# Q and K in seven output tiles, K's last four heads through the padding rows

## The chip, the core and the metric

The kernel runs on one NeuronCore of a Trainium2 chip. The metric is the device time of one execution in microseconds. The engines are TensorE (PE in the profile, with its weight loads as PEld), VectorE (DVE), ScalarE (ACT), GpSimd (POOL) and SyncE (SP), which issues most of the DMAs. Each engine works through its own queue in order and waits on semaphores of the others.

## The reference

A transformer block with conditioning, on 2048 tokens of width 448, in bf16:

```python
mod = (silu(c) @ w_mod)                 # six vectors: sa, ca, ga, sb, cb, gb
h = layernorm(x) * (1 + ca) + sa
# attention: 16 heads of 28; each token looks at 8 keys, itself and every second one before it
q, k, v = split(h @ wqkv)
o = softmax(q . k[pos - 2*w], w = 0..7) . v
x = x + ga * (o @ wo)
h = layernorm(x) * (1 + cb) + sb
x = x + gb * (silu(h @ w1) @ w2)        # 448 -> 1792 -> 448
```

## The kernel before

The 2048 tokens are cut into four chunks of 512 (256 positions of each parity, since attention looks only at keys of a token's own parity). Each chunk goes through layer norm, a transpose, Q, K and V projections, attention in blocks of 112 queries per parity (0 to 8, with 128 in block 0), the output projection, a second layer norm, and the two matrix products of the feed-forward part.

The code first records operations, each with a name, its engine, its dependencies and the buffers it takes, in a `Plan`; then it emits them in an order written out by hand, the string `ORDER`, in which a number is the operation's place of recording and a letter chooses ACT (`a`) or DVE (`v`) where either will do. Each engine's queue is the subsequence of `ORDER` that runs on it, so the order decides who stands behind whom. Names used here: `n1.2 T` is the transpose of chunk 2's first norm, `QK2.0.1` group 1 of chunk 2's Q and K, `V5` the values of block 5, `L3.0` the logits of block 3, parity 0, `exp` and `mask` what follows them, `AV3` attention times values, `onorm3` its division by the sums, `oT3` the transpose of the result, `WO1.0` the output projection, `x1` the residual add, `F1.0.2` tile pair 2 of chunk 0's first feed-forward product, `F2.0` a pair of rows of the second.

PSUM is used as four pairs of banks (`ps`). A projection takes one pair; a logits block takes two, and each is given back by its exp.

The contraction is over 448 = 3.5 x 128 rows. The helper `duo` fills two output tiles at once, with seven steps of two matmuls of 64 rows each that run side by side in the two halves of the array: three steps, then, after a `turn` (a wait on POOL's queue so that the halves may swap banks), four more, as two operations on PE. An eviction on ACT or DVE follows.

For Q and K a head's 28 columns are padded to 32, so that four heads fill the 128 rows of an output tile: rows 28 to 31 of every 32 are zero weights. Group g of 4 has a tile of Q and one of K (line 627), both evicted by one copy (line 630) into `qk`, whose dimensions are rows, Q or K, group, parity and position:

```python
w = wp[rows, kk, H * j + 4 * g:H * j + 4 * g + 4, :] if kk < 3 else wp3[rows, 4 * g:4 * g + 4, :]
return T.matmul(ps[:, j, 0:2 * n], lhsT=w.rearrange("p h d -> p (h d)"), rhs=h[rows, :, t, c0:c0 + n], start=start, stop=stop)
```

Chunk 0 comes in two parts of 256 columns, so that it can start early; the others have 512 columns. The padded weights `wp`, `wp3` are made by four `pad` copies from the loaded `wqk`, `wqk3` (lines 564 and 566). The space of `wqk` becomes later the normalised input of chunk 2, and `wqk3` and a part of `both` are scratch for sums of squares.

x of chunk 0 is loaded in two halves, `x0a` on SP's queue and `x0b` on ACT's; `c` follows on ACT's queue (line 368 issues all loads).

Of the kernel before, what the change touches and what calls it, by code (L numbers as in the profile page):

```python
# [15 lines left out]
D = 448  # L16
# [60 lines left out]
def half(j):  # L77
    return slice(K3 * j, K3 * j + K3)
# [33 lines left out]
def dram(ap, row, col, dims):  # L112

    w = ap.ap[0][0]
    return bass.AP(ap.tensor, ap.offset + row * w + col, [[r * w + c, n] for r, c, n in dims])

# [125 lines left out]
def layer(ctx, tc, io, safe):  # L242
# [13 lines left out]
    def ct(shape, name, dt=BF16):  # L256
        return const.tile(shape, dt, name=name)
# [15 lines left out]
    wp3 = ct([128, H, 32], "wp3")  # L273
    wo = ct([128, 2, KT, D], "wo")
# [16 lines left out]
    screp = ct([128, KT, 128], "screp")  # L291
# [78 lines left out]
    def first_x(i):  # L370
        return dict(out=x_all[:, 2 * i:2 * i + 2, :].rearrange("p t d -> p (t d)"), in_=x_view[0, :, i, :])
# [6 lines left out]
    ld_x = [[load(224, **first_x(0), run=1792, name="x0a"), load(224, **first_x(1), run=1792, q=nc.scalar, name="x0b")]]  # L378
    first = ld_x[0][0]["deps"][0]
    ld_c = [load(1, c4[0:3, :], c[:, 0:384].rearrange("o (k p) -> (o k) p", p=128), [ld_x[0][1]["deps"][0]], run=256, q=nc.scalar, name="c")]  # L380
# [11 lines left out]
    ld_qk = [[a], [b], [a], [load(56, wqk3[half(a), 0:D], A_wqkv[128 * (a + 1):128 * (a + 1) + K3, D * (1 - a):D * (2 - a)], late, name="wqk") for a in range(2)]]  # L392
# [6 lines left out]
    ld_1 += [load(112, w13[half(a), :], B_w1[128 * (a + 1):128 * (a + 1) + K3, F // 2 * (1 - a):F // 2 * (2 - a)], late, run=1792, name="w1") for a in range(2)]  # L399
# [161 lines left out]

    def pad(o, kk):
        if kk < 3:
            copy_on(o)(out=wp[:, kk, :, 0:DH], in_=wqk[:, kk, :].rearrange("p (h d) -> p h d", d=DH))
        else:
            copy_on(o)(out=wp3[:, :, 0:DH], in_=wqk3[:].rearrange("p (h d) -> p h d", d=DH))
# [28 lines left out]
    def norm1(k):  # L595
        h = h1[k % NH]
        after = [x for kk in (k - NH,) if kk >= 0 for x in qk_mm[kk] + v_mm[kk] + [halo[kk + 1]]] + (pads if k == 2 else [])
        if k == 0:
            parts = []
            for i in range(2):  # L600
                n = Norm([2 * i, 2 * i + 1], {2 * i + j: [ld_x[0][i]] for j in range(2)}, how=HOW1[0], tag=f"n1.0{i}")
                n.on_pe(lambda kk, i=i: h[:, :, kk, 128 + 128 * i:256 + 128 * i], [mod1])
                h1_norms.extend(n.done)
                parts.append(list(n.done))
            h1_done[0] = parts
            return
        n = Norm([4 * k + j for j in range(4)], {4 * k + j: [ld_x[k][j // 2]] + h1_norms[:1] for j in range(4)}, after=after, how=HOW1[k], tag=f"n1.{k}")
        n.on_dma(lambda j: h[:, :, :, 128 + 64 * j:256 + 64 * j].rearrange("p t k s -> p (t k) s"), lambda kk: h[:, :, kk, 128:128 + CP], 0, [mod1])
        h1_done[k] = [list(n.done)]
        w = 32 * k  # L610
        halo[k] = P.op(either(60.0 + 0.83 * 8 * w, 60.0 + 0.26 * 8 * w), lambda o: copy_on(o)(out=h[:, :, :, 128 - w:128].rearrange("p t k s -> p (t k) s"),
                                                                                           in_=h1[(k - 1) % NH][:, :, :, 128 + CP - w:128 + CP].rearrange("p t k s -> p (t k) s")),
                       h1_done[k - 1][-1] + after, name=f"halo{k}")

    def project(k):
# [3 lines left out]
        n = CP // len(parts)  # L619
        for i, ready in enumerate(parts):  # L620
            c0 = 128 + n * i
            s0 = CP * k + n * i
            done = []
            for g in range(4):
                def make(ps, j, kk, rows, t, start, stop, g=g, c0=c0):
                    w = wp[rows, kk, H * j + 4 * g:H * j + 4 * g + 4, :] if kk < 3 else wp3[rows, 4 * g:4 * g + 4, :]
                    return T.matmul(ps[:, j, 0:2 * n], lhsT=w.rearrange("p h d -> p (h d)"), rhs=h[rows, :, t, c0:c0 + n], start=start, stop=stop)  # L627

                def ev(o, ps, g=g, s0=s0):
                    copy_on(o)(out=qk[:, :, g, :, s0:s0 + n], in_=ps[:, :, 0:2 * n].rearrange("p j (t s) -> p j t s", t=2))  # L630
                m, e = duo(make, 2 * n, ready + pads, (either(act_ns(4 * n), dve_ns(4 * n)), ev, [], None), f"QK{k}.{i}.{g}")
                qk_mm[k] += m
                done.append(e)
            qk_done[k].append(done)
# [111 lines left out]
    def out_proj(k, i):  # L746
# [26 lines left out]
        for par in range(2):  # L773
            x1_done[u + par] = P.op(("dve", 545.0), lambda o, par=par: add(o, par), [m], name=f"x1.{u + par}")
# [224 lines left out]
```

## Time and profile before

| what | before |
|---|---|
| median of 3 runs (lowest to highest) | 171.43 us (171.3 to 171.44) |
| profiled execution | 171.64 us, span 169.9 us |
| PE busy | 162.0 us, 2015 matmuls |
| ACT busy | 114.5 us, 163 instructions |
| DVE busy | 96.1 us, 189 instructions |
| POOL busy | 33.2 us, 88 instructions |
| mean granted TensorE clock | 0.989 |

The span runs from the first instruction to the last. Busy time is the time in which an engine has an instruction in work; a matmul waiting inside its pipeline counts as busy, so a busy PE need not be at its full rate. A row of the timeline gives the start in the span, the length from the first start to the last end, the engine, the line, the operation, the tile written and the tiles read, the count, and in brackets the idle time before it with what ended it. Two rows of pipelined instructions can overlap at their ends, so the cost of a group is read from its start to the start of the next group.

### The profile page before, as it was taken

To read this page: it belongs to the slowest core of one execution; us is meant where nothing else is said; L and a number is where in the kernel's file an instruction comes from. 1 tells how busy PE (TensorE), PEld (TensorE's weight loads), DVE (VectorE), ACT (ScalarE), POOL (GpSimd) and SP (SyncE) were. 2 spreads that over 40 slices of the span, in tenths; PEclk is the share of its full clock that TensorE was granted. 3 is DMA by queue.
4 is the path that set the end of the run, shared out by engine and by line. 5 is a ranking of instruction groups with operands and counts; after the bars stand their busy time and mean duration, and the time that the engine had idled before them with its cause. 6 is when DMAs were issued, how large, how long until landed. Compare 5 with 4: busy or idle time off the path is not lost.

```text
span 169.9 us, 4812 instructions
## 1 busy us (share of the span) xinstructions
PE 162.0 (95%) x2015; PEld 83.9 (49%) x2015; DVE 96.1 (57%) x189; ACT 114.5 (67%) x163; POOL 33.2 (20%) x88
## 2 busy tenths in 40 slices
PE   7799999899999999999999999999999999999990
PEld 2258644545554564455644544655544444445450
DVE  4777999899979963895352577732473000000451
ACT  3148999999876889999878998662767862420000
POOL 7342424730502221132000205120150000000000
PEclk9959999999999999999999999999999999999999
DMA  4994448489979874022020030086008000000031
GB/s 142 289 326 165 99 94 314 78 202 242 176 185 252 177 198 106 0 66 46 20 54 0 4 90 22 2 112 178 6 10 224 0 4 0 0 4 0 38 136 64
DMA packets 32054, 17.51 MB, mean 103 GB/s; under 512 B 23896, under 2 KB 31640, under 8 KB 32024
## 3 DMA queue, kind: packets, MB, share of 16 engines
q1 hardware_dynamic: 31872, 16.90, 39.9%
q8 instruction: 17, 0.28, 0.7%
q10 hardware_dynamic: 152, 0.23, 0.5%
q14 instruction: 13, 0.11, 0.2%
HBM read 9.12 MB, written 1.84 MB: 64 GB/s over the span
## 4 chain that ended last, share of the span: by engine, by line
PE 75%; ACT 10%; DMA 6%; issue 3%; DVE 2%; POOL 1%; ACTq 0%; POOLq 0%
PE ps L791 25%; PE ps L808 22%; PE ps L627 7%; PE ps L753 6%; PE ps L638 5%; ACT p L678 4%; PE ps L730 4%; DMA wqk<-in_A_wqkv_dram 3%; PE ps L832 3%; PE ps L670 3%; DMA x_all<-in_A_x_dram 2%; ACT h L536 2%; ACT qk L630 1%; POOL rs L487 1%; ACT both L480 1%
## 5 line engine op out<-in xcount | busy, mean ns | idle before, releaser
L791 PE MATMUL ps<-h,w 64*128 64x512 bf16 x392 | 44.7, 376 | 0.0
L808 PE MATMUL ps<-w,both 64*128 64x448 bf16 x392 | 39.9, 349 | 0.0
L794 ACT ACTIVATE both<-ps 128x1024 bf16<-128x1024 f32 x28 | 27.3, 1023 | 13.9 <-PE ps L791 13.8
L678 ACT ACTIVATE p<-ps 128x896 bf16<-128x896 f32 (+1 forms) x36 | 31.5, 928 | 3.3 <-PE ps L670 3.2
L791 PEld LDWEIGHTS <-w 64*128 64x128 bf16 x392 | 19.5, 94 | 21.6
L808 PEld LDWEIGHTS <-both 64*128 64x128 bf16 x392 | 18.9, 94 | 17.7
L823 DVE TENSOR_TENSOR ot<-ps,x_all 128x896 bf16<-128x896 f32 x7 | 7.6, 1088 | 34.6 <-PE ps L808 34.3
L627 PE MATMUL ps<-h,wp 64*128 64x256 bf16 (+1 forms) x224 | 20.4, 323 | 0.6 <-ACT h L536 0.4
L627 PEld LDWEIGHTS <-wp 64*128 64x128 bf16 x280 | 13.9, 94 | 11.3 <-issue 1.1
L704 DVE TENSOR_TENSOR p<-p,maskb 128x1792 bf16<-128x1792 bf16 (+1 forms) x18 | 19.3, 1098 | 0.0
L768 DVE SCALAR_TENSOR_TENSOR x_all<-ps,x_all 128x448 bf16<-128x448 f32 x16 | 9.3, 618 | 9.7 <-PE ps L753 9.7
L487 POOL TENSOR_TENSOR rs<-rs,negh 128x2 f32<-128x2 f32 x16 | 13.8, 861 | 1.3
L753 PE MATMUL ps<-wo,oT 64*128 64x448 bf16 x112 | 13.0, 350 | 0.0
L480 ACT ACTIVATE wqk<-x_all,mv 128x448 bf16<-128x448 bf16 x16 | 10.7, 667 | 3.2 <-POOL mv L477 3.0
L477 POOL TENSOR_SCALAR mv<-sums 128x2 f32<-128x2 f32 x10 | 4.8, 479 | 40.0 <-DVE x_all L768 22.2
L638 PE MATMUL ps<-wv,h 64*128 64x448 bf16 x98 | 11.3, 350 | 0.2
L557 DVE TENSOR_SCALAR h<-h,modc 128x512 bf16<-128x512 bf16 x19 | 6.8, 408 | 6.6 <-DMA h<-xn 6.6
L630 ACT CAST qk<-ps 128x1024 bf16<-128x1024 f32 (+1 forms) x12 | 10.0, 871 | 0.7 <-PE ps L627 0.7
L321 ACT ACT_TABLE_LOAD x8 | 10.3, 1283 | 0.1
L486 POOL TENSOR_SCALAR rs<-mv 128x2 f32<-128x2 f32 x10 | 3.6, 356 | 33.3 <-ACT wqk L480 14.5
L736 DVE TENSOR_TENSOR o<-ps,rc 112x896 bf16<-112x896 f32 (+1 forms) x9 | 9.8, 1091 | 0.4
L501 DVE TENSOR_SCALAR xn<-x_all,mv,rs 128x512 bf16<-128x512 bf16 x23 | 8.8, 406 | 1.7 <-POOL rs L487 1.7
(84 smaller groups left out, 161.8 us busy)
## 6 DMA issues: line engine op xcount, KB each, us to landing
out_dram<-ot SPq DMA_DIRECT2D x7, 224.0 KB, 2.2
both<-in_w_mod_dram SPq DMA_DIRECT2D x2, 672.0 KB, 6.0
x_all<-in_A_x_dram SPq DMA_DIRECT2D x3, 448.0 KB, 7.0
w<-in_B_w_dram SPq DMA_DIRECT2D x3, 448.0 KB, 4.2
w<-in_B_w_dram SPq DMA_DIRECT2D x1, 896.0 KB, 5.3
both<-in_w_mod_dram SPq DMA_DIRECT2D x2, 336.0 KB, 5.8
w<-in_B_w_dram SPq DMA_DIRECT2D x1, 672.0 KB, 5.4
wqk<-in_A_wqkv_dram SPq DMA_DIRECT2D x1, 448.0 KB, 5.7
```

The source lines that it names most:

```text
L321: P.load = lambda t: S.preload_act_table(ACTF.Exp if t == "e" else ACTF.Silu)
L480: S.activation(out=scratch[late], in_=x_all[:, us[j], :], func=ACTF.Square, bias=mv[:, j, 0:1], accum_out=mv[:, j, 1:2])
L487: G.tensor_tensor(out=rs[:, j:j + n], in0=rs[:, j:j + n], in1=negh[:, 0:n], op=ALU.pow)
L627: return T.matmul(ps[:, j, 0:2 * n], lhsT=w.rearrange("p h d -> p (h d)"), rhs=h[rows, :, t, c0:c0 + n], start=start, stop=stop)
L630: copy_on(o)(out=qk[:, :, g, :, s0:s0 + n], in_=ps[:, :, 0:2 * n].rearrange("p j (t s) -> p j t s", t=2))
L638: return T.matmul(ps[:, j, 0:D], lhsT=h[rows, j, t, b0:b0 + 128], rhs=wv[rows, t, :], start=start, stop=stop)
L678: S.activation(out=out_, in_=ps[:, :, 0:4 * nq].rearrange("p j (g q) -> p j g q", q=nq), func=ACTF.Exp, scale=SCALE)
L704: V.tensor_tensor(out=p, in0=p, in1=maskb[:, 1 if b == 0 else 0, 0:nq].unsqueeze(1).to_broadcast([128, H, nq]), op=ALU.mult)
L753: return T.matmul(box["ps"][:, j, 0:D], lhsT=oT[rows, j, kk, s0:s0 + 128], rhs=wo[rows, j, kk, :], start=start, stop=stop)
L791: return T.matmul(ps[:, j, :], lhsT=w, rhs=h[rows, :, t, :], start=start, stop=stop)
L794: S.activation(out=hid[:, k % 2, :, i, :], in_=ps[:], func=ACTF.Silu)
L808: return T.matmul(box["ps"][:, par, 0:D], lhsT=hid[rows, k % 2, f % 2, f // 2, 128 * (2 * i + par):128 * (2 * i + par) + 128], rhs=w2[rows ...
```

## The change

Chunks 1 to 3 compute Q and K in seven output tiles in place of eight. The 112 columns of K's last four heads are spread over the padding rows of the seven others: seven tiles have 4 x 4 padding rows each, 112 in all. Groups 0 to 2 run as before, with both tiles. Group 3 has only Q's tile, whose 512 columns are split into two halves of 256 that take the places of the two tiles in `duo`. After the evictions four DMAs per chunk (`mv`), one for each 32 rows, move four padding rows of seven tiles to the 28 rows of K's group 3. The logits of a chunk depend on these DMAs too.

The weights for the padding rows are put there by nine copies on POOL (`fill`), six of which write into `wp` and `wp3` and so come after all of chunk 0's QK matmuls, which still use the zero padding. A few columns are loaded a second time, by two small loads into `wx`, since the two halves of the contraction have the tiles in other rows. Q's last tile as two halves needs a second arrangement of some weight rows, `wq3`. All QK matmuls of chunks 1 to 3, the transposes of chunk 2 (which overwrite `wqk`) and the first output adds wait for the fills.

Beside that: `x0b` is on SP's queue, behind `x0a`; `c` on ACT's queue no longer follows `x0b`; the two loads of `wqk3` are one, and the two of `w13` are one; `screp` lies in `both`. `ORDER` is another throughout: on ACT and DVE other evictions change places, all four pads are on DVE, V2, V3 and QK of chunk 2 come before AV1, and the logits of blocks 2 to 4 come after QK of chunk 2.

```diff
+    wq3 = ct([128, 2, 4, 32], "wq3")
+    wx = both[:, 12288:12288 + 3 * 112].rearrange("p (a n) -> p a n", n=112)
-    ld_x = [[load(224, **first_x(0), run=1792, name="x0a"), load(224, **first_x(1), run=1792, q=nc.scalar, name="x0b")]]
+    ld_x = [[load(224, **first_x(0), run=1792, name="x0a")]]
     first = ld_x[0][0]["deps"][0]
-    ld_c = [load(1, c4[0:3, :], ..., [ld_x[0][1]["deps"][0]], run=256, q=nc.scalar, name="c")]
+    ld_x[0].append(load(224, after=[first], **first_x(1), run=1792, name="x0b"))
+    ld_c = [load(1, c4[0:3, :], ..., run=256, q=nc.scalar, name="c")]
...
+    ld_q3 = [load(56, wx[:, 0:2, :], dram(A_wqkv, 128, 2 * D - 112, ((1, 0, 128), (64, -D, 2), (0, 1, 112))), late, run=224, name="wx"),
+             load(28, wx[:, 2, :], pairs_of(A_wqkv, 128, D - 112, 256, 2 * D - 112, 112), late, run=224, name="wx")]
...
+    def spread(ap, t0, t1):
+        return bass.AP(ap.tensor, ap.offset + t0, [list(ap.ap[0]), [1, t1 - t0], [DH, 4], [7, 4]])
+
+    def fill(out_, m0, in_, t0, t1, deps, name="fill"):
+        to = out_[:, m0:m0 + 4 * (t1 - t0), DH:32].rearrange("p (t r) c -> p t r c", r=4)
+        return P.op(("pool", 300.0), lambda o: G.tensor_copy(out=to, in_=spread(in_, t0, t1)), deps, name=name)
...
+    def move(r, s0, n, deps):
+        return sp(500.0, lambda o: nc.sync.dma_start(out=qk[32 * r:32 * r + DH, 1, 3, :, s0:s0 + n], in_=qk_t[32 * r + DH:32 * r + 32, 0:7, :, s0:s0 + n]), list(deps), 1700.0,
+                  kb=28.0, run=512, name="mv")[0]
...
-            for g in range(4):
+            for g in range(4 if k == 0 else 3):
...
+            if k:
+                def make(ps, j, kk, rows, t, start, stop, c0=c0):
+                    w = wq3[rows, kk // 3] if j and kk in (1, 3) else wp[rows, kk, 12:16, :] if kk < 3 else wp3[rows, 12:16, :]
+                    return T.matmul(ps[:, j, 0:n], lhsT=w.rearrange("p h d -> p (h d)"), rhs=h[rows, :, t, c0 + n // 2 * j:c0 + n // 2 * j + n // 2], start=start, stop=stop)
+                def ev(o, ps, s0=s0):
+                    copy_on(o)(out=qk[:, 0, 3, :, s0:s0 + n].rearrange("p t (j s) -> p j t s", j=2), in_=ps[:, :, 0:n].rearrange("p j (t s) -> p j t s", t=2))
+                m, e = duo(make, n, ready + pads + fills, (either(act_ns(2 * n), dve_ns(2 * n)), ev, [], None), f"QK{k}.{i}.3")
+                qk_mm[k] += m
+                done.append(e)
+                done = done + [move(r, s0, n, done) for r in range(4)]
```

More of the change, by code (lines that the diff above doesn't have):

```diff
@@ L115, in dram, with pairs_of @@
     return bass.AP(ap.tensor, ap.offset + row * w + col, [[r * w + c, n] for r, c, n in dims])
+def pairs_of(ap, r0, c0, r1, c1, n):
+    w = ap.ap[0][0]
+    return bass.AP(ap.tensor, ap.offset + r0 * w + c0, [[(r1 - r0) * w + c1 - c0, 2], [w, 64], [1, n]])
 class Plan:
@@ L290, in layer @@
     scT = ct([128, KT], "scT")
-    screp = ct([128, KT, 128], "screp")
+    screp = both[:, 12800:12800 + KT * 128].rearrange("p (k n) -> p k n", k=KT)
     scratch = (both[:, KT * 6 * D + 512:KT * 6 * D + 512 + D], wqk3[:])
@@ L374, in rows_of @@
         return ap.rearrange("(k p) n -> p k n", p=n)
-    ld_x = [[load(224, **first_x(0), run=1792, name="x0a"), load(224, **first_x(1), run=1792, q=nc.scalar, name="x0b")]]
+    ld_x = [[load(224, **first_x(0), run=1792, name="x0a")]]
     first = ld_x[0][0]["deps"][0]
-    ld_c = [load(1, c4[0:3, :], c[:, 0:384].rearrange("o (k p) -> (o k) p", p=128), [ld_x[0][1]["deps"][0]], run=256, q=nc.scalar, name="c")]
+    ld_x[0].append(load(224, after=[first], **first_x(1), run=1792, name="x0b"))
+    ld_c = [load(1, c4[0:3, :], c[:, 0:384].rearrange("o (k p) -> (o k) p", p=128), run=256, q=nc.scalar, name="c")]
     ld_c.append(load(1, c4[3:4, :], c[:, D - 128:D], [ld_c[0]["deps"][0]], run=256, q=nc.scalar, name="c"))
@@ L391, in layer @@
     b = load(224, wqk[:, 1, :].rearrange("p (a n) -> p a n", a=2), dram(A_wqkv, 128, 0, ((1, 0, 128), (64, D, 2), (0, 1, D))), late, name="wqk")
-    ld_qk = [[a], [b], [a], [load(56, wqk3[half(a), 0:D], A_wqkv[128 * (a + 1):128 * (a + 1) + K3, D * (1 - a):D * (2 - a)], late, name="wqk") for a in range(2)]]
+    ld_qk = [[a], [b], [a], [load(112, wqk3[:], pairs_of(A_wqkv, 128, D, 256, 0, D), late, name="wqk")]]
+    ld_q3 = [load(56, wx[:, 0:2, :], dram(A_wqkv, 128, 2 * D - 112, ((1, 0, 128), (64, -D, 2), (0, 1, 112))), late, run=224, name="wx"),
+             load(28, wx[:, 2, :], pairs_of(A_wqkv, 128, D - 112, 256, 2 * D - 112, 112), late, run=224, name="wx")]
     ld_v = [load(224, wv[:, 2 * a:2 * a + 2, :], dram(A_wqkv, 192 * a, 2 * D, ((1, 0, 128), (128, 0, 2), (0, 1, D))), late, name="wv") for a in range(2)]
@@ L398, in layer @@
     ld_1.append(load(448, w1[:, 1, :].rearrange("p (a n) -> p a n", a=2), dram(B_w1, 128, 0, ((1, 0, 128), (64, F // 2, 2), (0, 1, F // 2))), late, run=1792, name="w1"))
-    ld_1 += [load(112, w13[half(a), :], B_w1[128 * (a + 1):128 * (a + 1) + K3, F // 2 * (1 - a):F // 2 * (2 - a)], late, run=1792, name="w1") for a in range(2)]
+    ld_1.append(load(224, w13[:], pairs_of(B_w1, 128, F // 2, 256, 0, F // 2), late, run=1792, name="w1"))
     ld_2 = [load(112.0 * (f1 - f0), w2[:, f0:f1, :], B_w2[128 * f0:128 * f1, :].rearrange("(f p) d -> p f d", p=128), late, name="w2") for f0, f1 in ((0, 8), (8, NF))]
@@ L596, in norm1 @@
         h = h1[k % NH]
-        after = [x for kk in (k - NH,) if kk >= 0 for x in qk_mm[kk] + v_mm[kk] + [halo[kk + 1]]] + (pads if k == 2 else [])
+        after = [x for kk in (k - NH,) if kk >= 0 for x in qk_mm[kk] + v_mm[kk] + [halo[kk + 1]]] + (pads + fills if k == 2 else [])
         if k == 0:
@@ L613, in norm1 @@
                        h1_done[k - 1][-1] + after, name=f"halo{k}")
+    fills = []
+    qk_t = qk[:].rearrange("p j g t s -> p (j g) t s")
+    def move(r, s0, n, deps):
+        return sp(500.0, lambda o: nc.sync.dma_start(out=qk[32 * r:32 * r + DH, 1, 3, :, s0:s0 + n], in_=qk_t[32 * r + DH:32 * r + 32, 0:7, :, s0:s0 + n]), list(deps), 1700.0,
+                  kb=28.0, run=512, name="mv")[0]
     def project(k):
@@ L619, in project @@
         n = CP // len(parts)
+        if k == 1:
+            K3C = 2 * D - 112
+            fills.append(P.op(("pool", 700.0), lambda o: G.tensor_copy(out=wq3[:, :, :, 0:DH], in_=wx[:, 1:3, :].rearrange("p a (h d) -> p a h d", d=DH)), ld_q3, name="fill"))
+            fills.append(fill(wq3[:, 0], 0, wqk[:, 1, K3C:], 3, 4, ld_qk[1]))
+            fills.append(fill(wq3[half(0), 1], 0, wqk3[half(0), D - 112:], 3, 4, ld_qk[3]))
+            for out_, m0, in_, t0, t1, deps in ((wp[:, 0], 0, wqk[:, 0, K3C:], 0, 7, ld_qk[0]), (wp[:, 1], 0, wx[:, 0, :], 0, 4, ld_q3[0:1]), (wp[:, 1], 16, wqk[:, 1, K3C:], 4, 7, ld_qk[1]),
+                                                (wp[:, 2], 0, wqk[:, 2, K3C:], 0, 7, ld_qk[2]), (wp3[half(1)], 0, wx[half(1), 2, :], 0, 4, ld_q3[1:2]),
+                                                (wp3[half(0)], 0, wqk3[half(0), D - 112:], 4, 7, ld_qk[3])):
+                fills.append(fill(out_, m0, in_, t0, t1, deps + qk_mm[0] + pads))
+            wmod_read.extend(fills)
         for i, ready in enumerate(parts):
@@ L630, in ev @@
                     copy_on(o)(out=qk[:, :, g, :, s0:s0 + n], in_=ps[:, :, 0:2 * n].rearrange("p j (t s) -> p j t s", t=2))
-                m, e = duo(make, 2 * n, ready + pads, (either(act_ns(4 * n), dve_ns(4 * n)), ev, [], None), f"QK{k}.{i}.{g}")
+                m, e = duo(make, 2 * n, ready + pads + fills, (either(act_ns(4 * n), dve_ns(4 * n)), ev, [], None), f"QK{k}.{i}.{g}")
                 qk_mm[k] += m
                 done.append(e)
+            if k:
[8 more added lines that the diff above has]
+                done = done + [move(r, s0, n, done) for r in range(4)]
             qk_done[k].append(done)
@@ L773, in out_proj @@
         for par in range(2):
-            x1_done[u + par] = P.op(("dve", 545.0), lambda o, par=par: add(o, par), [m], name=f"x1.{u + par}")
+            x1_done[u + par] = P.op(("dve", 545.0), lambda o, par=par: add(o, par), [m] + (fills if k == 0 else []), name=f"x1.{u + par}")
         P.op(("none", 0.0), none, [x1_done[u], x1_done[u + 1]], give=((a, "ps"),))
```

43 rows, old and new, of the table ORDER are left out of this document.

## The prediction

> **What bounds the kernel now.** I read the page's busy line first, then what TensorE (PE) waits for, then PE's timeline, then ScalarE (ACT), and last the DMA rows.
>
> ```profile
> span 169.9 us, 4812 instructions
> PE 162.0 (95%) x2015; PEld 83.9 (49%) x2015; DVE 96.1 (57%) x189; ACT 114.5 (67%) x163; POOL 33.2 (20%) x88
> ```
>
> The profiled run took 171.64 us, 1.74 more than its span and 0.21 above the median of 171.43. I sum against 171.64 and take 0.2 off at the end.
>
> All that PE waited for:
>
> ```profile
> PE ps L529 <- DVE xn L501: 1.3, 1, 1.3
> PE ps L405 <- DVE both L339: 1.2, 1, 1.2
> PE ps L670 <- DVE o L736: 0.5, 1, 0.5
> PE ps L627 <- ACT h L536: 0.4, 1, 0.4
> ```
>
> PE's timeline (start, length, then the group):
>
> ```profile
> 12.73 1.59 PE L627 MATMUL ps<-h,wp 64*128 64x256 bf16 x26
> 14.69 2.91 PE L627 MATMUL ps<-h,wp 64*128 64x256 bf16 x50 [0.36 <-ACT h L536]
> ...
> 30.80 0.96 PE L730 MATMUL ps<-v,p 128*128 128x29 bf16 x32
> 31.61 0.92 PE L450 MATMUL ps<-both,screp 128*128 128x448 bf16 x4
> ...
> 34.01 0.37 PE L670 MATMUL ps<-qk 28*128 28x112 bf16 x14 [0.51 <-DVE o L736]
> ...
> 72.35 7.76 PE L791 MATMUL ps<-h,w 64*128 64x512 bf16 x70
> 79.93 2.83 PE L808 MATMUL ps<-w,both 64*128 64x448 bf16 x28
> ...
> 118.33 4.70 PE L808 MATMUL ps<-w,both 64*128 64x448 bf16 x48
> 122.87 0.81 PE L791 MATMUL ps<-h,w 64*128 64x512 bf16 x6
> ...
> 160.50 5.47 PE L832 MATMUL ps<-w,both 128*128 128x448 bf16 x28
> ```
>
> The last wait ends at 34.01; from there PE runs without a gap to 165.97, and the tail is an add and a store that the change leaves alone. Prices: 70 matmuls (35 pairs) of 512 columns take 79.93 - 72.35 = 7.58, so a pair costs 0.216; 24 pairs of 448 take 122.87 - 118.33 = 4.54, so 0.189; 13 pairs of 256 take 1.59 less a tail of some 0.17, so 0.109. An AV block is 0.9, a logits block 0.35, the gate 0.78.
>
> From 12.73 to 34.01 PE is not dense, though it is shown busy. Its work there is QK of chunk 0 (56 pairs, 6.1), QK of chunk 1 (28 pairs of 512, 6.05), V0 and V1 (14 pairs, 2.65), four logits blocks (1.4), two AV (1.8) and the gate (0.78): 18.8 of 21.3 us, so 2.5 idle. So two stages: a start of 34 us that waits, and 132 us of pure PE work.
>
> **The change, part by part.**
>
> *Fewer matmuls.* Chunks 1 to 3 each lose the eighth output tile: of eight tiles of seven half-row matmuls, six stay, and Q's last runs as two halves of 256 columns. 28 pairs of 512 become 21 of 512 and 7 of 256: 7 x (0.216 - 0.109) = 0.75 per chunk, 2.25 in all.
>
> *Evictions.* Each chunk also drops half an eviction (1024 to 512 columns), some 0.4 of ACT or DVE.
>
> ACT's rows:
>
> ```profile
> 10.66 0.94 ACT L564 COPY wp<-wqk 128x896 bf16<-128x896 bf16 x1 [4.07 <-DMA wqk<-in_A_wqkv_dram]
> 11.79 2.85 ACT L536 ACTIVATE h<-ps,modc 128x256 bf16<-128x256 bf16 x6 [0.19 <-DVE h L538]
> 29.50 3.73 ACT L630 CAST qk<-ps 128x1024 bf16<-128x1024 f32 x4
> 36.15 0.91 ACT L642 CAST v<-ps 128x896 bf16<-128x896 f32 x1
> 67.64 1.28 ACT L321 ACT_TABLE_LOAD   x1
> 76.49 4.74 ACT L794 ACTIVATE both<-ps 128x1024 bf16<-128x1024 f32 x5
> 94.05 3.35 ACT L678 ACTIVATE p<-ps 128x896 bf16<-128x896 f32 x4
> ```
>
> An exp follows the next at (3.35 - 0.92) / 3 = 0.81, a QK eviction at 0.91, a first-FFN eviction at 0.93.
>
> *Start-up.* c goes first on ACT's queue, and x0b moves behind x0a on SP's; the bytes ahead of the projection weights are the same, so ACT's 10.66 stays. ACT's pad goes to DVE, so ACT's modulations need not follow it to 11.79, and one of the four modulations also goes to DVE. QK of chunk 0 still starts near 12.75, but I expect the 0.36 wait to go. Merged weight loads: nothing; x0b's 0.4 is covered by DVE still doing x0a's statistics.
>
> *Fills.* Nine POOL copies. Six write into the padding of the weights that chunk 0 still reads, so they start only when its QK ends, near 18.9, and all QK of chunk 1 is behind them; with the copy of wx, seven are on that path. Meanwhile the new order lets PE do V1, V0, L0.0, L0.1, the gate and V3's first part: 2.65 + 0.7 + 0.78 + 0.57 = 4.7, with waits for banks 5.8, to 24.7. For the fills:
>
> ```profile
> L357 POOL TENSOR_SCALAR_AFFINE_SELECT maskb<-maskb 128x256 bf16<-128x256 bf16 x1 | 0.4, 407 | 0.1
> ...
> 35.24 1.16 POOL L490 TENSOR_TENSOR nm<-mv,rs 128x2 f32<-128x2 f32 x1 [2.30 <-PE ps L638]
> 36.49 0.26 POOL L492 TENSOR_SCALAR nm<-nm 128x2 f32<-128x2 f32 x1
> ...
> 35.27 1.08 DVE L879 TENSOR_TENSOR wo<-wo,gbc 128x1792 bf16<-128x1792 bf16 x1
> ```
>
> Clean, I take 0.25 each (a third to all of the affine row's elements), 1.8 in all, and POOL has an rstd (about 1) among them: done by 22 to 24.5, hidden. The upper end is 1.16 each, 8 us, as where POOL ran beside DVE's wo multiply. [...]
>
> *Start, summed.* To 34.4 I have the new order finish chunk 0's QK (6.1), chunk 1's (5.3), V0 to V3 (5.3), four logits (1.4), AV0 (0.9), the gate (0.78): 19.8 of 21.65, so 1.9 idle against 2.5: -0.6. Both ends: 1.0 idle (-1.5) and 3.5 (+1.0).
>
> *The order from 34 on.* Where the old order spreads twelve exps between two chunks' projections (34 to 59 us), the new one does all of QK2 and then L2.0 to L4.1 close together. There are four bank pairs; a logits block holds two until its exps are done (0.81 each). Walking the order with the rows' durations I get PE waits of 0.25 before AV1 (bank of QK2's last ACT eviction), 0.4 before WO0.0 (second exp of L2.0), 0.25 before L3.0, 0.1 at the modulation matmuls, 0.2 before QK3: +1.2. At the first FFN, two evictions, a table load (1.28) and four exps in a row cost 0.15 before its third tile and 0.3 around AV5: +0.45. Bounds: 0, since the old order has no PE wait here, and 0.4 before each of six logits blocks, 2.4, with 0.9 at the FFN.
>
> *Moves.* Twelve DMAs on SP, four per chunk, behind the chunk's last eviction; logits of the chunk wait for them.
>
> ```profile
> both<-in_w_mod_dram SPq DMA_DIRECT2D x2, 672.0 KB, 6.0
> wo<-wo SPq DMA_DIRECT2D x1, 224.0 KB, 5.3
> h<-xn SPq DMA_TRANSPOSE x12, 2.7
> oT<-o SPq DMA_TRANSPOSE x9, 3.1
> ...
> 36.38 0.51 SPq L882 DMA_DIRECT2D wo<-wo  x1
> ...
> 34.00:40.00 6.00, 5.87 (x92) 2.68 (x93) 5.97 (x11) 5.82 (x11) 1.63 (x3) 1.00 0.99 222
> ...
> 40.00:50.00 10.00, 10.00 (x158) 5.55 (x154) 9.59 (x16) 8.42 (x13) 2.15 (x4) 1.00 0.99 187
> ```
>
> (The last two rows are stretches of the span: busy time of PE, weight loads, DVE, ACT, POOL, then clock, DMA share and GB/s.)
>
> An issue takes 0.5 to 0.6. Chunk 1's moves issue from 32.8 to 34.9, ahead of L2.0 at 39.7. Chunk 2's can go at 41, with two w_mod loads between them: six issues, the last starting near 43.9, ahead of L4.0 at 48.4. Landing takes 2.7 (a transpose) to 6.0 (the big load); I take 3.1, since oT's transposes move as little, in the same stretch. So both are hidden, by 1.7 and 1.4. At 6.0 they are late by 0.7 and 1.5. Chunk 3's have some 8 us in hand. Queued behind them on SP: the wo copy (wanted at 42, issued by 35.5, lands by 41 at 5.3), oT0, chunk 3's transposes (wanted at 46), and oT1 behind chunk 2's (issued 44.5, wanted at 52): hidden. Attention's x1 adds also wait for the fills, long done.
>
> *Sum.* -2.25 - 0.6 + 1.2 + 0.45 = -1.2: 170.4 on the profiled run's scale, 170.2 on the median's.
>
> **The rivals.**
>
> *Dense again* (20%): the new order costs PE no wait after 34, as the old one: -2.25 - 0.6 = -2.85, 168.6. For it: ACT and DVE each lose 1.2 us of evictions. Against: ACT is then 5.82 of 6 and 8.42 of 10 us busy.
>
> *Moves late* (24%), the other side: in 34 to 40 us the DMA engines are 0.99 busy. If the moves land after 6.0, L2.0 and L4.0 stall for 0.7 + 1.5 = 2.2; with the 1.2 gained that is 1.0 slower, 172.4, up to 172.9 if the dense logits stage adds more. It decides from 1.5 us of lateness in all. [...]
>
> [...]
>
> **How the numbers follow.** My forecast has 40% (169.2 to 171.0). No change and a measurable one part at about 0.2%, 0.34 us. Faster: the forecast, nearly all (0.38), and dense (0.20): 0.58. Same: the rest of the forecast, a third of late fills, and a little of late moves: 0.11. Slower: 0.31. The range, 168.6 to 172.8, runs from the dense case to late moves and leaves out a tenth at each end.
>
> **What would show it.** Right: 21 pairs of 512 and 7 of 256 per chunk; PE's chunk 0 projection without the wait for ACT h; QK of chunk 1 released by h, not POOL; waits of some 1.2 us in all between QK2 and QK3, released by ACT p; no PE wait on a DMA into qk. Wrong: PE waiting on qk moves before L2.0 or L4.0, POOL copies of 1 us before QK of chunk 1, or a PE with no waits after 35 us.

## The result and the profile after

The changed kernel takes 180.88 us at the median (177.7 to 182.9, 4 runs), the kernel before 171.37 in the same job: 1.0448 times as long, 95% interval 1.0318 to 1.0578. It is slower, and outside the predicted range. The profiled run took 180.26 us with a span of 178.5, so it stands for the median. Most ratios here, and the table of four versions below, leave out disturbed runs, those over 1.5% above the fastest of their kernel, while medians keep them, so the two can differ by a per cent.

The page of the changed kernel, and from its view of waits all that PE waited for longest:

```profile
span 178.5 us, 4831 instructions
PE 162.1 (91%) x2014; PEld 84.7 (47%) x2015; DVE 95.9 (54%) x193; ACT 112.2 (63%) x159; POOL 32.7 (18%) x97
...
PE ps L725 <- DMA qk<-qk: 4.8, 3, 3.7
PE ps L447 <- DMA both<-in_w_mod_dram: 1.8, 2, 1.3
PE ps L846 <- POOLq L322: 1.3, 1, 1.3
...
PE ps L543 <- DVE xn L515: 1.1, 1, 1.1
```

PE's waits add up to 11.3 us, against 3.4 before. The largest is the one the prediction named as the sign of its failing: logits (L725) behind a DMA into `qk`. The waits for POOL's queue (L322 is the `turn`) and for `w_mod` are new.

PE's timeline of the changed kernel, at the start of chunk 0's projection, before L2.0, before L4.0, what follows that, and the first feed-forward product:

```profile
14.26 7.19 PE L670 MATMUL ps<-h,wp 64*128 64x256 bf16 x112
...
43.86 0.22 PE L725 MATMUL ps<-qk 28*128 28x112 bf16 x2 [0.83 <-DMA qk<-qk]
...
56.10 0.22 PE L725 MATMUL ps<-qk 28*128 28x112 bf16 x2 [3.73 <-DMA qk<-qk]
56.25 0.96 PE L447 MATMUL ps<-scT,both 128*128 128x1 bf16 x32
57.08 1.65 PE L464 MATMUL ps<-both 128*128 128x448 bf16 x4
...
60.76 0.38 PE L725 MATMUL ps<-qk 28*128 28x112 bf16 x16
...
85.59 1.69 PE L846 MATMUL ps<-h,w 64*128 64x512 bf16 x14 [1.26 <-POOLq L322]
...
168.48 5.47 PE L887 MATMUL ps<-w,both 128*128 128x448 bf16 x28
```

PE ends at 173.95, before at 165.97: +8.0. The projection of chunk 0 starts 1.5 later (14.26 for 12.73) and takes 7.0 (to 21.29) where its 56 pairs are worth 6.1. The gate at 57.08 takes 1.65 where it took 0.92 before. In both places the clock is low. Two stretches of the changed kernel, then one of the kernel before, with the granted clock third from the end of the row:

```profile
9.10:15.90 6.80, 5.22 (x62) 3.76 (x65) 4.45 (x16) 2.64 (x6) 1.90 (x5) 0.50 0.89 299
56.90:60.30 3.40, 3.40 (x55) 2.03 (x53) 1.98 (x7) 1.79 (x5) 0.00 (x0) 0.50 1.04 325
```

```profile
9.30:12.70 3.40, 3.30 (x21) 1.65 (x17) 2.85 (x11) 1.85 (x3) 1.09 (x3) 0.50 1.00 337
```

TensorE ran at half clock for 6.8 us at the start, where the kernel before has 3.4, and for 3.4 us just after the longest wait. From the gate to L4.1 (57.08 to 60.76) that is 3.7 us; the same three groups at full clock take 2.5 in a run shown below (57.19 to 59.70, clock 1.00 from 55 to 60 us). So the clock costs 1.2 us there. At the start it adds nothing to the projection itself: the kernel before took 7.0 for the same 56 pairs, from 12.73 to 20.43 less a group of logits and the wait of 0.36. Its clock was full by then (1.00 from 12.7 to 20.43), but PE made short stops that the profile doesn't count as waits. The rows of the kernel before that end this stretch:

```profile
17.52 0.40 PE L670 MATMUL ps<-qk 28*128 28x128 bf16 x16
17.86 2.64 PE L627 MATMUL ps<-h,wp 64*128 64x256 bf16 x36
20.43 0.49 PE L670 MATMUL ps<-qk 28*128 28x128 bf16 x16
```

The start, in DVE's timeline, of the changed kernel and of the one before: the pad of the fourth projection weight, `wqk3`.

```profile
10.66 0.28 DVE L591 COPY wp<-wqk 128x448 bf16<-128x448 bf16 x1 [4.28 <-DMA wqk<-in_A_wqkv_dram]
10.86 0.41 DVE L515 TENSOR_SCALAR xn<-x_all,mv,rs 128x512 bf16<-128x512 bf16 x1
```

```profile
7.75 0.38 DVE L501 TENSOR_SCALAR xn<-x_all,mv,rs 128x512 bf16<-128x512 bf16 x1
8.84 0.28 DVE L566 COPY wp<-wqk 128x448 bf16<-128x448 bf16 x1 [0.71 <-DMA wqk<-in_A_wqkv_dram]
```

The pad waits for the merged load of `wqk3` and comes 1.8 later. With that load split it comes at 9.54, so 1.1 of this is the merging; SP also issues the first of these loads at 2.85 instead of 2.48, behind `x0b`, and the rest was not taken apart. In the new order the pad stands ahead of the norm, so the norm that PE's transposes need waits too. Last, the moves. From the chain of waits, issue and landing of the last move of chunks 1 and 2; from SP's timeline, their issues; from the DMA view of 34 to 45 us, the engines' share in slices of 0.28 us:

```profile
36.95 6.86 DMA qk<-qk
50.25 5.81 DMA qk<-qk
```

```profile
34.64 2.97 SPq L645 DMA_DIRECT2D qk<-qk  x4
```

```profile
DMA  5475899994221221268994222111499111121999
```

Landing takes 5.8 to 6.9 us, and for the greater part of the 6.9 (36.95 to 43.81) the DMA engines are one to two tenths busy, with two bursts between: in that part the bytes are not waiting for full engines. By my estimate 0.1 to 0.2 is as much as two or three of the 16 fully at work. Besides the moves, `w13`, issued at 32.68, may be landing there; no row shows when it does.

The difference in PE's end, summed over all rows of PE's timeline, each group from its start to the start of the next and with the waits taken out: waits +7.9; Q and K of chunks 1 to 3 −2.9 (16.2 instead of 19.1); all other groups together +3.0. That makes the measured 8.0. Of the 3.0 the half clock after L4.0 is 1.2. The other 1.8 is spread over transposes, V, logits, the output projection and the first feed-forward product, and no run separates its causes.

### The profile page after: what moved, and what is told of

The parts are those of the page before. It is cut to its first block, busy times and chain, and to the rows that moved or that the text cites. A ratio compares the mean times of both kernels' runs of the same rounds, so it can differ in the third digit from the quotient of the medians.

```text
span 178.5 us, 4831 instructions
## 1 busy us (share of the span) xinstructions
PE 162.1 (91%) x2014; PEld 84.7 (47%) x2015; DVE 95.9 (54%) x193; ACT 112.2 (63%) x159; POOL 32.7 (18%) x97
## 4 chain that ended last, share of the span: by engine, by line
PE 70%; DMA 11%; ACT 5%; SPq 4%; DVE 4%; POOL 2%; issue 1%; POOLq 0%; DVEq 0%
PE ps L846 23%; PE ps L863 21%; DMA qk<-qk 7%; PE ps L670 6%; PE ps L808 6%; DMA wqk<-in_A_wqkv_dram 4%; PE ps L785 3%; PE ps L887 3%; PE ps L693 3%; SPq L645 2%; PE ps L725 2%; ACT p L733 2%; SPq L378 2%; DVE qk L673 1%; POOL rs L500 1%; PE ps L464 1%
## 5 line engine op out<-in xcount | busy, mean ns | idle before, releaser
L846 PEld LDWEIGHTS <-w 64*128 64x128 bf16 x392 | 19.1, 94 | 23.8 <-POOLq L322 1.8
L670 PE MATMUL ps<-h,wp 64*128 64x256 bf16 (+1 forms) x196 | 17.8, 326 | 0.0
L670 PEld LDWEIGHTS <-wp 64*128 64x128 bf16 x238 | 12.3, 97 | 6.7 <-issue 0.4
L725 PE MATMUL ps<-qk 28*128 28x112 bf16 (+1 forms) x288 | 8.1, 211 | 5.5 <-DMA qk<-qk 4.8
L501 POOL TENSOR_TENSOR rs<-rs,negh 128x2 f32<-128x2 f32 x16 | 12.4, 773 | 1.3
L515 DVE TENSOR_SCALAR xn<-x_all,mv,rs 128x512 bf16<-128x512 bf16 x26 | 9.8, 407 | 4.3 <-POOL rs L501 4.3
L491 POOL TENSOR_SCALAR mv<-sums 128x2 f32<-128x2 f32 x10 | 3.2, 344 | 47.8 <-PE ps L846 28.5
L571 DVE TENSOR_SCALAR h<-h,modc 128x512 bf16<-128x512 bf16 x20 | 7.4, 410 | 6.4 <-DMA h<-xn 6.4
L725 PEld LDWEIGHTS <-qk 28*128 28x128 bf16 x288 | 4.5, 92 | 12.1 <-issue 6.5
L500 POOL TENSOR_SCALAR rs<-mv 128x2 f32<-128x2 f32 x10 | 4.9, 494 | 28.2 <-PE ps L808 10.7
```

Source lines behind the costliest of these rows:

```text
L501: G.tensor_tensor(out=rs[:, j:j + n], in0=rs[:, j:j + n], in1=negh[:, 0:n], op=ALU.pow)
L725: T.matmul(held[t][:, j, g * nq:(g + 1) * nq], lhsT=key, rhs=q, start=True, stop=True)
L846: return T.matmul(ps[:, j, :], lhsT=w, rhs=h[rows, :, t, :], start=start, stop=stop)
```

## Experiments

Medians of all runs, and the ratio to the kernel before with its interval where one was given. Runs of one variant spread by up to 5 us where those of the kernel before stay within 2.5, so differences under some 2 us decide nothing.

**Merged loads: together, apart, and in the old kernel.** Theory A: the loss is the three `pairs_of` loads (their first dimension is a pair of blocks of 64 rows), each on few DMA engines (the shares of one to two tenths above). Theory B: it is the moves.

```diff
-load(224, w13[:], pairs_of(B_w1, ...), late, ...)        # one DMA, outermost dimension 2
+load_two(224, w13, [B_w1[128:192, F//2:F], B_w1[256:320, 0:F//2]], late, ...)  # two DMAs of 64 partitions
```

The first has this for `wqk3`, `wx` and `w13`, the second for `w13` alone, the third for `wqk3` alone; the fourth is the kernel before with `wqk3` and `w13` merged and nothing else.

> The changed kernel with its three merged loads (wqk3, w13, the second of wx) issued as two DMAs of 64 partitions each, as the kernel before does for two of them; nothing else differs. Theory A, the merged loads: their outermost dimension is 2 and they drain on about two of the sixteen DMA engines (share 1 to 2 tenths from 37 to 41 us in the changed kernel's trace), so wqk3 lands at 10.66 instead of 8.84 and the moves stand behind w13. Then the wait before QK of chunk 0 goes (-1.5), L2.0 no longer waits for a move (-1.0), L4.0 hardly (-3.7) and the half clock after that wait goes (-1.3): 180.3 - 7.5 = 172.8, between 171.5 and 174. Theory B, the moves themselves: few source partitions and a place behind a 672 KB load make them late whatever the loads do. Then only the start is won: 177.5 to 179, and L4.0 still waits 2.5 us or more.

> Only w13 split in two DMAs. Theory A: wait of L2.0 (1.0) gone, that of L4.0 smaller, start unchanged (QK of chunk 0 at 14.3): 174 to 177. Theory B: L2.0 and L4.0 wait as before, 179 to 181.

> Only wqk3 split in two DMAs. Both theories: the first pad on DVE comes at about 8.9 instead of 10.66, QK of chunk 0 starts near 12.8 instead of 14.26, the half clock of the start is shorter; 1.5 to 2.5 faster than the changed kernel if nothing later takes it back (178 to 179). If the moves' lateness is set by when loads are done and not by when QK of chunks 1 and 2 is done, the gain is lost again at L4.0 (180).

> The kernel before with its two wqk3 loads merged into one and its two w13 loads merged into one, as the changed kernel has them, in the same order otherwise. Theory A: wqk3 lands 1.5 to 2 later; in this order DVE has the first norm ahead of that pad, so the start loses 0.5 to 1.5; the w13 load of about 5 us on two engines delays the wo copies and oT0 behind it, up to 2: 172 to 175. Theory B: the same time as before within 0.5 (171.4).

Measured: 176.79 (1.0211, 1.0084 to 1.0339), 176.04, 179.11 (1.0449, 1.036 to 1.0538), and 177.36 (1.035, 1.0241 to 1.0458). The second met its theory A and the third about what was expected of it; the first lies between its two theories, the fourth above its theory A. PE's waits of the kernel before with merged loads, and a stretch of it:

```profile
PE ps L541 <- DVE xn L513: 3.6, 3, 2.3
PE ps L765 <- DMA oT<-o: 1.8, 1, 1.8
...
54.50:57.50 3.00, 2.71 (x24) 0.89 (x20) 3.00 (x8) 1.78 (x5) 0.47 (x3) 1.00 0.13 51
```

Splitting gives back about 4 of 9.5 us, all of it from `w13`. More telling, merging two loads costs the old kernel 4 to 7 us with no move and no seventh tile in it (runs of 175.62, 176.15, 178.57 and 178.75; 5.6 at the median). The profile is of the 175.62, and two waits account for its 4: 2.3 more of waiting for the norm (the pieces of it behind the pad, which waits for `wqk3` until 10.40), and a wait of 1.8 for a transpose. SP issued `w13` at 49.63 and the next load at 50.26, and from 54.5 to 57.5 the DMA engines are 0.13 busy (next to last in the row); the transpose lands at 59.05. So theory A's cause holds, for a part of the loss. With all three split, none of PE's waits names a move, but the kernel is still some 4 to 5 slower than before.

The share fits theory A: after `w13` here 0.13 of 16 engines are busy, and 0.20 from 36 to 39 us in a version below, after the moves. From 34 to 45 us, 19 of the 40 slices of the changed kernel are at 0.1 or 0.2, and 7 in the version with `w13` split. Over how many engines a DMA was spread, no view shows.

**The moves, with and without the merged loads.**

```diff
-sp(500.0, lambda o: nc.sync.dma_start(out=qk[32*r:32*r+DH, 1, 3, ...], in_=qk_t[32*r+DH:32*r+32, 0:7, ...]), ...)
+sp(500.0, lambda o: None, ...)                      # and qk[:, 1, 3, :, CP:] set to 0 once
```

> The changed kernel without its twelve moves: K's heads 12 to 15 of chunks 1 to 3 stay at zero (cleared once at the start), so that part of the computation is left out; the merged loads and the order stay. Theory A (the moves' late landing costs what PE waits for it, 4.8 us, and the half-clock piece that follows the second wait, another 0.8): 174.5 to 176, with no half clock near 57 and the start as in the changed kernel (projection of chunk 0 from about 14.3). Theory B (the moves' waits only stand in front of other waits, banks and ACT, which take their place): 178 to 180.

> The changed kernel with its three merged loads split and without its twelve moves: K's heads 12 to 15 of chunks 1 to 3 stay at zero, so that part of the computation is left out. With the split version alone (176.8) it gives the moves' price in the order of the change. Theory A (the moves hold up what stands behind them): 172.5 to 174. Theory B (the order itself, with w_mod loads issued late and its matmuls early, costs most): 175 to 176.5.

The first is the changed kernel, the second the one with its loads split. With the two above they make a square (means, us; the kernel before was 171.3 to 171.9 in these jobs; the ratios are in brackets, and the two medians without moves are 178.45 and 172.35):

| | loads merged | loads split |
|---|---|---|
| with moves | 179.0 (1.0448, 1.0318 to 1.0578) | 175.4 (1.0211, 1.0084 to 1.0339) |
| without moves | 178.3 (1.0411, 1.0351 to 1.047) | 172.1 (1.0028, 0.9994 to 1.0063) |

The merged loads cost 3.5 with the moves and 6.2 without; the moves 3.3 with split loads, and 0.7 with merged ones, which is not clear of the spread. Each hides part of the other, and for the moves in the changed kernel theory B of the first run is the better (178.45 in its 178 to 180): without them other waits take their place. PE's waits there (changed kernel without moves):

```profile
PE ps L448 <- DMA both<-in_w_mod_dram: 3.9, 3, 2.6
PE ps L544 <- DVE xn L516: 2.3, 1, 2.3
```

Of the second, theory A's 172.5 to 174 was about right (172.35). The corner without both is the rest of the change, fewer matmuls, fills and order: it comes out even with the kernel before, and not 1.2 better.

**The clock at the start.**

```diff
-for _ in range(JUNK): ... warm_up(w_last, 2)
+for i in range(JUNK): ... warm_up(w_last, 9 if i == 2 else 2)   # on the version with split loads
```

> The version with all three merged loads split, and seven more warm-up matmuls in the place where PE waits for the modulation weights (7.4 to 8.7 us), which changes no result. Theory A (the half clock from 9.4 to 16.2 is brought on by PE's idle time before it): the two pieces of 3.4 us go or shrink to one, the 112 matmuls of chunk 0 take 6.2 to 6.7 us in place of 7.85, and the whole is 1 to 1.7 below the split version (176.8 at the median): 175.1 to 175.8. Theory B (the half clock comes at that time whatever PE did before): no change, 176.5 to 177.

Measured 177.14 (1.0261, 1.0201 to 1.0321). At the start it is as theory A has it; the total is not. The version with split loads has a clock of 0.50 from 10 to 15 us and 0.88 from 15 to 20. With seven more warm-up matmuls, in the same stretch as above and in the timeline of PE:

```profile
9.10:15.90 6.80, 5.56 (x95) 4.09 (x95) 5.80 (x20) 4.06 (x10) 2.53 (x8) 1.00 0.87 299
```

```profile
13.54 6.22 PE L676 MATMUL ps<-h,wp 64*128 64x256 bf16 x110 [0.17 <-ACT h L556]
...
52.03 0.22 PE L731 MATMUL ps<-qk 28*128 28x112 bf16 x2 [2.72 <-DMA qk<-qk]
```

Full clock, and chunk 0's projection ends at 19.59 where the version with split loads has 20.81. But the total does not move: PE comes 1.1 earlier to L4.0 (48.94 for 50.06) and waits 2.72 there for the moves, the last of which lands 1.5 later than in the version with split loads. From the chain of waits of this version, and from the weight loads of the one with split loads:

```profile
47.34 4.64 DMA qk<-qk
```

```profile
50.55 0.09 PEld L731 LDWEIGHTS <-qk 28*128 28x128 bf16 x2 [0.28 <-DMA qk<-qk]
```

Behind the 2.72 here the granted clock is 0.91 from 50 to 55 us and 0.75 from 55 to 60. In the version with split loads it is 0.88 and 0.78 there, and PE's only wait from 44 to 60 us is 0.45. How much idle time brings the half clock on, these runs don't show.

**Start order, and the turn on POOL.**

```diff
-... 28 65 81 92 77v 72 82v 71 83v 84 85 73 29 ...       # pad of wqk3 (77) ahead of the norms (82, 83)
+... 28 81 92 82v 84 83v 85 93v 95 71 77v 94v 96 65 72 73 29 ...
-... 544 505 157 155 450 451 448 ...                     # second rstd of n2.1 (544) ahead of a turn (451)
+... 505 157 155 450 451 544 448 ...
```

> The version with all three merged loads split, and two parts of the order changed: at the start DVE takes the norms of chunk 0 before its pad of the fourth projection weight, and PE the transposes before the modulation matmuls; on POOL the second rstd of the norm of the second chunk's FFN stands behind the next turn, not ahead of it. Theory A (the start loses 1.5 us to the late pad and to half clock, the first FFN 1.4 to the turn): the projection of chunk 0 begins near 12.7 and ends near 19.5, no wait for POOL in the first FFN, 173.5 to 174.5. Theory B (a wait removed there comes back at the next, because ACT and DVE are as late): 175.8 to 177.

Measured 175.05 (1.019, 1.0135 to 1.0245), between the theories. The wait for POOL is gone, which shows its cause: in the changed kernel the `turn` stood behind this row of POOL's timeline, a 128x2 operation of 2.46 us, where the median of its line is 0.19, while DVE masked and multiplied (82.27 to 85.43).

```profile
83.02 2.46 POOL L500 TENSOR_SCALAR rs<-mv 128x2 f32<-128x2 f32 x1 [2.61 <-PE ps L846]
```

The start was a miss in the profiled run. With norms and transposes first, PE idled before and between them, the half clock lasted longer (0.52 from 15 to 20 us, against 0.88 with split loads alone), and the projection took 9.17 (this is the longest of the four runs, 177.6 at a mean clock of 0.961; the others took 173.6 to 175.2 at 0.98, so their start may have been better):

```profile
9.91 0.61 PE L548 MATMUL ps<-ident,xn 128*128 128x128 bf16 x4 [1.39 <-DVE xn L520]
...
14.10 9.17 PE L675 MATMUL ps<-h,wp 64*128 64x256 bf16 x112 [1.01 <-ACT h L555]
```

**SP's order.** Two versions put the `w_mod` loads earlier: the first on top of the start order above, ahead of chunk 2's moves; the second on top of the warm start, ahead of the first `oT`, with the w1 load (53) behind the moves and the turn mended. The third is the second without moves.

```diff
-264 265 43 44 376 262 263 37 38 ... 268 ... 266 267 ... 367 368     # moves 264 262 268 266, w_mod 43 37, oT1 367
+43 44 37 38 264 265 367 368 376 262 263 ... 268 ... 266 267         # first
+43 44 37 38 349 ... 293 ... 295 ... 264 ... 262 ... 268 ... 266 ... 367 368 53 54   # second; oT0 349, h 293 295
```

> The last version, with SP's order changed as well: both w_mod loads of 672 KB ahead of the four moves of chunk 2, and the transposes of the second attention block's output behind the first move, not behind the fourth. Theory A (SP's order costs the wait for w_mod at the modulation matmuls, 1.5, and the one for oT, 0.5, with its piece of half clock): both waits go, 1.5 to 2.5 below the version before it, 171.5 to 172.5. Theory B (the moves then stand behind 1344 KB on the same engines): L4.0 waits 1 to 3 us for the moves of chunk 2, and nothing is gained.

> The version with split loads and seven more warm-up matmuls, with two parts of the order changed: on SP both w_mod loads of 672 KB in all and 112 KB stand ahead of the first oT transpose (issued near 38 in place of 44 to 46), and the w1 load of 448 KB behind the four moves of chunk 2, so that these are issued near 43 to 45 with little ahead of them; on POOL the second rstd stands behind the turn. Theory A (what PE waits for near 50 us, moves in one version and w_mod in another, is what SP issues from 42 to 48 and lands late, so one wait comes back as the other until both are issued early): neither wait stays, no half clock after 50, 171.0 to 173.0. Theory B (the DMA engines are full from 35 to 55 us whatever the order): PE waits 2 to 4 us for moves, w_mod or oT there, 175 to 177.

> The version before it without its twelve moves: K's heads 12 to 15 of chunks 1 to 3 stay at zero, so that part of the computation is left out. It gives the price of the moves where the loads around them are out of the way. Theory A (none, as their landing is hidden there): within 0.7 of the version with moves. Theory B (they still hold up logits or other transfers): 1.5 to 3 less.

Measured 178.27 (1.0382, 1.0306 to 1.0457), 177.17 (1.0333, 1.0262 to 1.0403), and without moves 171.58 (0.9998, 0.9958 to 1.0038). The first was to remove waits for `w_mod` and `oT`, but the version under it no longer had them (it waited 2.7 for moves). The wait for the moves fell to 1.8 (theory B's 1 to 3), chunk 0's projection began 0.6 later, and the whole rose by 3, more than these explain; its four runs have a mean clock of 0.960 to 0.971, so part of the rise may be the clock. (The two `w_mod` loads that change place are of 672 and 56 KB.) In the second no logits waited for moves and, after the start, nothing for `w_mod`, but PE stood 5.6 us at the output projection:

```profile
48.05 1.67 PE L814 MATMUL ps<-wo,oT 64*128 64x448 bf16 x8 [5.58 <-DMA oT<-o]
...
57.19 0.92 PE L470 MATMUL ps<-both 128*128 128x448 bf16 x4
...
59.70 0.38 PE L731 MATMUL ps<-qk 28*128 28x112 bf16 x16
```

SP's timeline and two stretches of it (DMA share next to last), then SP's timeline without the moves:

```profile
34.86 3.01 SPq L651 DMA_DIRECT2D qk<-qk  x4
...
38.50 1.23 SPq L378 DMA_DIRECT2D both<-in_w_mod_dram  x2
39.84 1.27 SPq L801 DMA_TRANSPOSE oT<-o  x1
41.22 6.18 SPq L570 DMA_TRANSPOSE h<-xn  x2
...
36.00:39.00 3.00, 3.00 (x38) 1.71 (x36) 2.12 (x3) 2.92 (x8) 1.51 (x4) 1.00 0.20 41
39.00:43.00 4.00, 3.39 (x82) 2.04 (x76) 3.77 (x6) 3.84 (x6) 0.20 (x1) 1.00 0.93 211
```

```profile
36.05 1.23 SPq L379 DMA_DIRECT2D both<-in_w_mod_dram  x2
37.91 1.25 SPq L802 DMA_TRANSPOSE oT<-o  x1
39.27 3.69 SPq L571 DMA_TRANSPOSE h<-xn  x2
```

Four moves hold SP 3.0 us, 0.75 each for 28 KB, and for three microseconds four fifths of the DMA time is unused. Everything behind them starts later: the `w_mod` loads at 38.5 for 36.05, and `oT` and `h`, which then stand behind 1.1 MB of loads, moves and the `wo` copy, finish so late that SP is held until 47.4. So in this order the moves cost 5.6 us, more than either theory gave, and not one logits block waits for them. Which wait shows is a matter of order.

**The order mended, and other queues for the moves.** The fourth has the `w_mod` loads behind chunk 2's moves and their matmuls (144, 142) behind QK3.0.1; the last two leave the order of the second and issue the moves from POOL or ACT.

```diff
-... 43 44 37 38 349 ...   ... 144 142 ... 145 ... 143 ...
+... 266 267 43 44 37 38 ...   ... 310a 144 145 142 143 ...
```

```diff
-nc.sync.dma_start(out=qk[...])
+nc.gpsimd.dma_start(out=qk[...])      # or nc.scalar
```

> The version with SP's w_mod loads ahead of the first oT transpose, with those loads put behind the four moves of chunk 2 instead, and the second modulation's matmuls and gate some 6 us later on PE (behind the second of chunk 3's QK tiles). Theory A (each wait near 45 to 55 us is a place in SP's order: a move or a large load ahead of what PE needs next): the 5.6 us wait for oT goes and no other takes its place, 171 to 173. Theory B (moves and loads together take longer than the stage has, in any order): 2 to 4 us of waits for moves, oT or w_mod, 174 to 176.

> The version with SP's w_mod loads ahead of the first oT transpose, with the twelve moves issued by POOL on its own queue in place of SP; nothing else is changed. Theory A (the moves cost by what they hold up behind them on SP and in its queue): the wait of 5.6 us for oT goes, as it does without moves, 171.5 to 173.5. Theory B (the moves' packets load the DMA engines themselves, whichever queue they come from): 175 to 177. POOL's own issue time may add waits for turns in both.

> The same with the moves issued by ACT on its own queue. Theory A: no wait for oT, but ACT loses some 0.6 us per issue, 2.4 per chunk, in a stage where it has little to spare: 173 to 175. Theory B: 176 to 178.

Measured 179.94 (1.0489, 1.0437 to 1.0541), 183.16 (1.0637, 1.0568 to 1.0707) and 178.34 (1.0413, 1.0346 to 1.048): the times of theory B or above in all three. The longest of PE's waits in each of the three, in this order:

```profile
PE ps L814 <- DMA oT<-o: 3.0, 1, 3.0
```

```profile
PE ps L731 <- DMA qk<-qk: 7.7, 3, 4.6
```

```profile
PE ps L731 <- DMA qk<-qk: 4.1, 4, 1.5
```

With the moves off SP the wait for `oT` goes, so SP's place was its cause; but then the logits wait 4.1 (ACT) or 7.7 (POOL, in the longest of its four runs) for the moves themselves: those of chunk 1, issued by ACT from 36.97 to 40.18, are waited for until 45.73. Some places keep the moves out of PE's waits, but none that I tried makes them free. Whether moves of another form would be hidden was not tried.

## Why the prediction was wrong

- **"Merged weight loads: nothing"** is the step that failed first. It priced a DMA by its bytes alone; the merging costs 3.5 to 6.2 us in the changed kernel, and the kernel before loses 4 to 7 by it alone.
- **"I take 3.1" for the moves' landing** failed: 5.8 and 6.9, so its upper bound of 6.0 was passed once too. I took the price of a transpose, by bytes, where it was a 28-row copy behind a merged load. The issue was taken at 0.5 to 0.6 and is 0.65 to 0.83. The rival, moves late, had place and sign right (L2.0, L4.0); it gave 2.2 us of waits, measured 4.8. By its own figures it should have given 2.7, since a landing of 6.0 after 34.9 is 1.2 behind 39.7, not 0.7.
- **"Queued behind them on SP: ... hidden"** failed where it was tested: the version with its moves on SP and an early `w_mod` lost 5.6 to just that. In the changed kernel itself PE waits for no `oT`.
- **The clock was in no term.** It is 1.2 of the 8.0 us: after the wait of 3.7 before L4.0 came 3.4 us at half clock.
- **Start, −0.6**: failed; the projection began 1.5 later, since I had DVE's pad of `wqk3` as free and its load on time.
- **The order from 34 on, +1.2 +0.45**: the bank waits it listed are mostly absent (0.7 and 0.2 in the profile). What came was a `turn` behind an rstd on POOL, 1.3, a queue the walk had left out.
- **Fewer matmuls, −2.25**: right, and too small: −2.9 by the rows, since Q and K in the kernel before also held about 1 us of short stops (19.1 where the prediction's prices give 18.1).
- **Fills hidden**: right. The seven on the path take 0.24 to 0.37 each, the last is done at 25.9, and QK of chunk 1 starts at 26.55 without a wait; no run shows the late fills that the chances count.
- With loads split, moves out and `w_mod` early, the rest of the change is at 171.58, no gain. By the same sum over PE's rows as above, Q and K save 2.8 there too (16.3 instead of 19.1), waits take back 0.8 (4.2 against 3.4), and the other groups 1.5, so PE ended only 0.48 earlier in the profile (165.49). Why the other groups take longer was not tested; so the forecast of a gain failed here on a term that the prediction doesn't have, and its cause is open.

## What to carry to other kernels

Don't price a DMA by its bytes alone: here merging two pairs of loads cost the old kernel 4 to 7 us, a move of 28 KB took 5.8 to 6.9 us to land, and where four moves held SP for 3.0 us, PE waited 5.6 for what stood behind them. When an extra DMA can't be dropped, ask what it delays, not only who waits for it; in version after version here the wait moved between moves, `w_mod`, `oT` and POOL while the time hardly fell. And idle time on TensorE can be paid twice: a wait of 3.7 us here was followed by half clock worth 1.2 more. Before adding up such costs, take the same rows from the kernel before: what looks lost to the clock at the start was lost there too, in another way.

## What was not expected of the hardware

Two pairs of small DMAs, each merged into one, cost 4 to 7 us in a kernel of 171. The clock dropped to half in the middle of the kernel after a wait of 3.7 us, for 3.4 us. A 128x2 operation on POOL took 2.46 us beside DVE, where the mean of its group is 0.49 and the median 0.19. And the variants vary by up to 5 us from run to run while the kernel before varies by 2.5 at most. The longer runs mostly have the lower mean clock (the kernel before with merged loads: 175.6 and 176.2 at 0.986 and 0.977, 178.6 and 178.8 at 0.970), so half clock is probably part of it; why it differs from run to run is open.
